# A planner that passes backward and forward over its plan, paced warm-up products, and a start cut into finer steps

## The chip, the cores and the metric

The kernel runs on one core of a Trainium2 chip. The metric is the device time of one execution in microseconds (us), the median of several. Names of engines: PE is TensorE (matrix products), DVE is VectorE, ACT is ScalarE, POOL is GpSimd, SP is SyncE, which here issues nearly all DMAs.

## The reference

Three layers follow each other. The first is a linear attention with a decaying state, for each batch and head; then come two expert layers on the same 3072 tokens of width 384.

```python
# r, k, v, w: [4, 8, 768, 48]; state: [4, 8, 48, 48]
for t in range(S):
    cur = einsum('bhd,bhe->bhde', u[None] * kt, vt)
    y[:, :, t] = einsum('bhd,bhde->bhe', rt, state + cur)
    state = wt[:, :, :, None] * state + einsum('bhd,bhe->bhde', kt, vt)
# x: the y of all heads side by side, [3072, 384]
x = (silu(x @ w_gate) * (x @ w_val)) @ w_out            # 384 -> 1536 -> 384
h = x @ w_in                                            # 384 -> 1024
solu = h * softmax(h)
x = (solu - mean) / sqrt(var + 1e-6) * g_ln @ w_out2    # 1024 -> 384
```

The expert weights arrive as 64-bit floats. The kernel turns them into 32-bit values on DVE and ACT, and splits weights and activations into a high and a low part (names with h and l: hg and lg, xh and xl, mh and ml), so that each product of matrices is three products on PE: high by high, high by low, low by high.

## The kernel before

**Attention.** The tokens are cut into 24 pieces, n = 0 to 23, of 128 tokens: piece n is token block q = n // 4 of batch b = n % 4, two chunks of 64 tokens each, all 8 heads. `att_prep(n)` (from line 455) records its steps.

- On DVE: a forward scan of w (L484), a reciprocal (L487), a backward scan (L489), then two multiplies of r and k with the results (L337, written to the tile `feat`). For pieces under NDG = 4 one more product r*k goes to the tile `PR` (L337), from r and k as they were before those multiplies. `PR` has one buffer, which all pieces share.
- On PE: `s_kt` transposes k (kT, L574) and, for pieces under 4, multiplies r*k with u in products of two columns (L576, the diagonal step) in the same step and the same PSUM bank; `s_qk` does k by r (QK, L527); `s_up` k by v (UP, L633); `s_av` the masked QK by v and r by the state (AV, L676 and L679). Pieces under NFLAT = 4 are *flat*: QK and UP are steps of their own, with one bank each, one mask product and one add to the state on DVE. From piece 4 on, QK and UP are one step over two banks, with three mask products and two adds.
- On ACT: the transposed k goes to `kt` (L340), the diagonal from PSUM to `dg` and, for pieces under NOWN = 4, eight products with it (L590, called own here), with pieces from NOWN to NDG on DVE.
- At the end PE transposes the result (yT, L726), and ACT and DVE split it into `xh` and `xl`.

**First expert layer.** `weights` loads and decodes two 128-column weight tiles at a time (steps L340, L376, L379, L382, L384); for the first two loads (NLO = 1) PE forms the low halves with the identity matrix (the corrections, L449 and L450). `moe1_unit` does a unit m of 128 of the 1536 columns for one token block: 9 products for gate, 9 for value, silu on ACT, the product on DVE, the split into `mh` and `ml`, and 9 products with w_out (L748 to L750). Units m < HM0 = 3 of block 0 and m < HM1 = 6 of block 1 run in two halves of 256 tokens, so that they can start when two pieces of four are ready; the others in one of 512.

**Second expert layer.** Products L1028 to L1030, then a softmax and a normalization on DVE and ACT, a transpose by DMA for most pieces, and products L1197 to L1199. `finish` copies each result from PSUM on ACT and stores it with a DMA from SP.

**What sets the order.** Nothing is issued as it is written. Every step goes into a `Graph` with an engine, an estimated duration, a priority (a due time) and its data; `emit` then plays the plan through once: each engine takes, of its steps that are ready by the estimates, the one with the smallest priority, and the instruction is issued at that moment. So the estimates and the due times fix each engine's order; on the chip an engine goes through its own order and waits where its data are not there. The due times come from the tables of numbers in line 63. While PE has nothing to do at the start, `fill` puts in products of the identity matrix with itself (L1234, the warm-ups); before, these are 13 products at the start.

Of the kernel before, what the change touches and what calls it, by code (L numbers as in the profile page):

```python
# [26 lines left out]
C = 64  # L27
# [14 lines left out]
NFLAT = 4  # L42
# [5 lines left out]
NOWN = 4  # L48
# [12 lines left out]
T0, ADV, ADV2, MARG = 15.0, 2.0, 12.0, 16.0  # L61
HM0, HM1 = 3, 6
ATS, PPS, OWS, DUS, DUD, UNS, SIS, FWS, FRS = {2: -2.0, 3: -1.0, 5: -8.0, 7: -3.0, 8: 4.0, 10: 5.0, 11: 1.0}, {0: 2.0, 1: 5.0, 2: -1.0, 4: 2.0, 5: -5.0, 6: 1.0, 7: 3.0, 9: 5.0, 10: -4.0, 11: 13.0}, {1: -29.0, 2: 2.0, 3: 5.0}, {1: -1.0, 2: 2.0, 6: -2.0, 7: -9.0, 8: -22.0, 9: -8.0, 10: -4.0, 11: 2.0, 12: 1.0, 14: 8.0, 16: -12.0, 17: -9.0}, {0: -12.0, 3: 10.0, 4: -3.0, 5: 14.0, 6: -5.0, 7: -7.0, 8: -22.0, 10: 12.0, 11: 6.0, 12: 7.0, 13: -2.0, 14: -14.0, 15: 3.0, 16: 41.0, 17: 1.0}, {0: 14.0, 1: 6.0, 2: -8.0, 3: -4.0, 4: 1.0, 6: 9.0, 7: 6.0, 9: -3.0}, {0: -9.0, 1: -5.0, 2: 10.0, 3: 9.0, 5: -16.0, 7: -27.0, 8: -4.0, 9: 16.0}, {3: 16.0, 4: 1.0, 5: -8.0, 7: 18.0, 8: -12.0, 9: -19.0}, {1: -31.0, 2: 2.0, 4: -2.0, 6: -1.0, 7: -1.0, 8: -8.0, 9: -1.0}
# [9 lines left out]
class Graph:  # L73
# [5 lines left out]
    FILL, FROM, UNTIL, WARM, IDLE = 0.235, 4.0, 8.4, 7.0, 2.2  # L79
    LAT = {"PE": 0.2, "ACT": 0.13, "DVE": 0.13, "POOL": 0.13, "DMA": 2.6, "ADMA": 2.6, "CTL": 0.0}  # L80

    def __init__(self):
        self.opts, self.prio, self.fn, self.deps = [], [], [], []
        self.last, self.readers = {}, {}
        self.port = set()
        self.fill = self.tiles = None
        self.takes, self.holds, self.bank_of, self.owner = {}, {}, {}, {}
# [52 lines left out]
    def emit(self):  # L140
        self.order_takes()
        n = len(self.opts)
        users = [[] for _ in range(n)]
# [11 lines left out]
        self.at, self.fills = [None] * n, []  # L155
        free = sorted(self.tiles)
        idle = [0.0]

        def fill(m, t):
            if not free or t < self.FROM or t > self.UNTIL and t < idle[0] + self.IDLE:  # L160
                return 0.0
            for _ in range(m):
# [29 lines left out]
        while events:  # L192
            t = events[0][0]
            while events and events[0][0] <= t:
                _, kind, i = heapq.heappop(events)
                if kind == 0:
                    for e in self.opts[i]:
                        heapq.heappush(ready.setdefault(e, []), (self.prio[i], i))
# [11 lines left out]
                else:  # L210
                    for j in users[i]:
                        same = taken[i] == "PE" and "PE" in self.opts[j]
                        ready_at[j] = max(ready_at[j], t + (0.0 if same else self.LAT[taken[i]]))
# [1104 lines left out]
```

## Time and profile before

| | us |
|---|---|
| timed runs | 742.65, 743.68, 746.32 |
| median | 743.68 |
| the profiled execution | 744.02 |
| its span | 741.9 |
| busy in the span: PE / DVE / ACT / POOL | 730.9 / 546.0 / 356.5 / 72.6 |

The profile is of one execution. The span goes from the first to the last instruction; the time of the execution has what lies around it. The busy time of an engine is a sum over stages with different limits, so it is read stretch by stretch. The granted clock of PE is given as a share of 2.4 GHz; the two levels seen are 1.00 and 0.50. A start in the order of time is in us from the span's start, the figure behind it is how long the instruction (or the merged group) took, and a bracket tells how long the engine was idle before it and what ended that.

### The profile page before, as it was taken

Reading aid. Unit: us, or ns where it says so; the run is one execution under the profiler, and the core shown is the slowest. Engines: PE = TensorE matmul, PEld = TensorE weight load, DVE = VectorE, ACT = ScalarE, POOL = GpSimd, SP = SyncE. Lnnn points to the kernel's source line nnn. Section 1 sums busy time; section 2 is a strip of 40 time slices with the busy share of each in tenths; the row PEclk is TensorE's granted clock in tenths of the full one; section 3 lists DMA queues with packets and bytes.
Section 4 is the critical chain, followed back from the end, with each engine's and each line's share of the span. In section 5 each row is a group of like instructions: output and inputs, shape, how many; then the busy total and the mean of one; then the engine's idle time right before and its main releaser. Section 6 shows DMA issues by size and latency. Waiting matters only on the chain.

```text
span 741.9 us, 15891 instructions
## 1 busy us (share of the span) xinstructions
PE 730.9 (99%) x6287; PEld 632.1 (85%) x6287; DVE 546.0 (74%) x1099; ACT 356.5 (48%) x698; POOL 72.6 (10%) x64
## 2 busy tenths in 40 slices
PE   6999999999999999999999999999999999999998
PEld 6798888999888888888888888888888889999998
DVE  7699999988877687766867537976344988778830
ACT  4797673634344333323434323564554465555551
POOL 0000000000000000000000000000024242543240
PEclk9699999999999999999999999999999999999999
DMA  9887642414333233333333125610324244343331
GB/s 266 255 250 222 222 142 82 137 47 130 106 116 106 60 85 103 115 91 89 96 88 123 47 57 143 198 43 12 89 58 149 64 122 116 88 114 96 86 106 43
DMA packets 62617, 84.63 MB, mean 114 GB/s; under 512 B 18896, under 2 KB 46288, under 8 KB 62544
## 3 DMA queue, kind: packets, MB, share of 16 engines
q1 hardware_dynamic: 62128, 83.52, 39.3%
q8 instruction: 49, 0.80, 0.5%
q14 instruction: 24, 0.20, 0.1%
q10 hardware_dynamic: 416, 0.10, 0.1%
HBM read 59.47 MB, written 9.44 MB: 93 GB/s over the span
## 4 chain that ended last, share of the span: by engine, by line
PE 99%; DMA 0%; issue 0%; DVE 0%; ACT 0%
PE ps L748 17%; PE ps L749 16%; PE ps L750 16%; PE hp L1028 4%; PE hp L1029 4%; PE hp L1030 4%; PE psa L748 4%; PE psa L750 4%; PE psa L749 4%; PE pc L1199 2%; PE pb L1199 2%; PE pb L1197 2%; PE pc L1197 2%; PE pb L1198 2%; PE pc L1198 2%; PE ps L676 2%
## 5 line engine op out<-in xcount | busy, mean ns | idle before, releaser
L748 PE MATMUL ps<-xh,hg 128*128 128x512 f32 (+1 forms) x348 | 130.5, 375 | 0.0
L750 PE MATMUL ps<-xh,lg 128*128 128x512 f32 (+1 forms) x348 | 128.9, 370 | 0.0
L749 PE MATMUL ps<-xl,hg 128*128 128x512 f32 (+1 forms) x348 | 128.8, 370 | 0.0
L337 POOL TENSOR_TENSOR tl<-xt,th 128x512 fp32r<-128x512 f32 x44 | 55.7, 1296 | 636.0 <-DVE ml L337 543.9
L340 ACT ACTIVATE mh<-sg 128x512 fp32r<-128x512 f32 (+1 forms) x81 | 47.1, 583 | 92.9 <-DVE sg L337 88.1
L748 PE MATMUL ps<-mh,ho 128*128 128x512 f32 (+1 forms) x243 | 90.0, 370 | 0.0
L749 PE MATMUL ps<-ml,ho 128*128 128x512 f32 (+1 forms) x243 | 88.9, 366 | 0.0
L750 PE MATMUL ps<-mh,lo 128*128 128x512 f32 (+1 forms) x243 | 88.9, 366 | 0.0
L748 PEld LDWEIGHTS ps<-xh,hg 128*128 128x128 f32 x348 | 65.6, 188 | 11.5
L750 PEld LDWEIGHTS ps<-xh,lg 128*128 128x128 f32 x348 | 65.6, 188 | 11.3
L749 PEld LDWEIGHTS ps<-xl,hg 128*128 128x128 f32 x348 | 65.6, 188 | 10.8
L785 ACT ACTIVATE sg<-ps 128x512 f32<-128x512 f32 (+1 forms) x57 | 32.1, 563 | 84.9 <-PE ps L750 82.8
L337 DVE TENSOR_TENSOR sg<-sg,ps 128x512 f32<-128x512 f32 (+1 forms) x59 | 37.2, 630 | 47.4 <-PE ps L750 46.4
L337 DVE TENSOR_TENSOR ml<-sg,mh 128x512 fp32r<-128x512 f32 (+1 forms) x81 | 50.4, 623 | 16.5 <-ACT mh L340 16.3
L1029 PE MATMUL hp<-i2l,xh 128*128 128x512 f32 x144 | 56.6, 393 | 0.0
L1028 PE MATMUL hp<-i2h,xh 128*128 128x512 f32 x144 | 56.5, 393 | 0.0
L1030 PE MATMUL hp<-i2h,xl 128*128 128x512 f32 x144 | 56.0, 389 | 0.0
L340 ACT ACTIVATE kt<-PR 32x256 f32<-32x256 f32 (+1 forms) x128 | 46.3, 361 | 17.3 <-DVE PR L600 15.8
L748 PEld LDWEIGHTS ps<-mh,ho 128*128 128x128 f32 x243 | 45.8, 188 | 7.5
L750 PEld LDWEIGHTS ps<-mh,lo 128*128 128x128 f32 x243 | 45.8, 188 | 7.4
L749 PEld LDWEIGHTS ps<-ml,ho 128*128 128x128 f32 x243 | 45.8, 189 | 7.2
L1040 DVE TENSOR_REDUCE sm<-hp 128x1 f32<-128x1024 f32 x24 | 29.3, 1221 | 29.8 <-PE hp L1030 29.8
(184 smaller groups left out, 1683.9 us busy)
## 6 DMA issues: line engine op xcount, KB each, us to landing
tok<-tok SPq DMA_DIRECT2D x20, 576.0 KB, 4.2
xt<-tb SPq DMA_DIRECT2D x176, 64.0 KB, 2.0
feat<-feat SPq DMA_DIRECT2D x24, 448.0 KB, 4.4
feat<-feat SPq DMA_DIRECT2D x24, 231.4 KB, 3.0
vv<-vv SPq DMA_DIRECT2D x24, 192.0 KB, 4.7
st<-w_gate SPq DMA_DIRECT2D x12, 384.0 KB, 5.2
st<-w_val SPq DMA_DIRECT2D x12, 384.0 KB, 5.9
st<-w_out SPq DMA_DIRECT2D x12, 384.0 KB, 4.1
```

Source lines behind the costliest of these rows:

```text
L337: return lambda: eng.tensor_tensor(out=out, in0=in0, in1=in1, op=op)
L340: return lambda: ACT.activation(out=out, in_=in_, func=AF.Copy)
L748: PE.matmul(out=o, lhsT=wh, rhs=xhi, start=first, stop=False, **kw)
L749: PE.matmul(out=o, lhsT=wh, rhs=xlo, start=False, stop=False, **kw)
L750: PE.matmul(out=o, lhsT=wl, rhs=xhi, start=False, stop=last, **kw)
L785: lambda: ACT.activation(out=sg, in_=pg.t[:, 0:n], func=AF.Silu), [pg.key], [sk]))
L1028: PE.matmul(out=hp()[:, f], lhsT=xh_[:, k, s], rhs=R["i2h"][:, k, f], start=(k == 0), stop=False)
L1029: PE.matmul(out=hp()[:, f], lhsT=xh_[:, k, s], rhs=R["i2l"][:, k, f], start=False, stop=False)
L1030: PE.matmul(out=hp()[:, f], lhsT=xl_[:, k, s], rhs=R["i2h"][:, k, f], start=False, stop=(k == KD - 1))
L1197: PE.matmul(out=po(), lhsT=th[:, m], rhs=R["o2h"][:, m], start=(m == 0), stop=False)
L1198: PE.matmul(out=po(), lhsT=th[:, m], rhs=R["o2l"][:, m], start=False, stop=False)
L1199: PE.matmul(out=po(), lhsT=tl[:, m], rhs=R["o2h"][:, m], start=False, stop=(m == M2 - 1))
```

## The change

- The planner. `emit` now makes a plan with the given due times (`run`), goes backward over it from its end (`late`: when must each step begin at the latest, with each engine doing one thing at a time), takes these times as new due times, and does so three times; the plan with the earliest planned end is issued. A DMA is planned as a time to be issued, then a place on a shared wire, then a landing.
- The warm-ups. The planner keeps an account of how much PE has done in the last stretch of the plan, with a weight for each kind of step (`cool`: 0.05 for the diagonal step, 0.35 to 0.55 for small products, 0.9 otherwise). Up to 60 us of the plan it puts a warm-up product in when the account is low and PE has nothing ready, and below a second bound it holds back a step that is ready and puts a warm-up first. There are now 18 warm-ups: 8 at the start, then 4, 1, 1, 2 and 2.
- The start. w of pieces 0 and 1 comes in two halves, each with a scan of its own. `PR` has two buffers, one for each parity of n. The diagonal step is a step of its own, with a bank of its own and a due time of its own.
- Numbers: NFLAT 4 to 5, NOWN 4 to 3, HM1 6 to 4, T0 15 to 17, and new tables of due times. PEV, ARO and NSH are 0, so what hangs on them emits nothing.
- The end. The result of the last piece is copied in two halves, on ACT and on DVE, and stored by two DMAs, from SP and from ACT.

```diff
-NFLAT = 4
+NFLAT = 5
-NOWN = 4
+NOWN = 3
-T0, ADV, ADV2, MARG = 15.0, 2.0, 12.0, 16.0
-HM0, HM1 = 3, 6
+T0, ADV, ADV2, MARG = 17.0, 2.0, 12.0, 16.0
+HM0, HM1 = 3, 4
+NSPL = 2
+PEV, ARO = 0, 0
+ROUNDS = 3
+NSH = 0
...
-    FILL, FROM, UNTIL, WARM, IDLE = 0.235, 4.0, 8.4, 7.0, 2.2
-    LAT = {"PE": 0.2, "ACT": 0.13, "DVE": 0.13, "POOL": 0.13, "DMA": 2.6, "ADMA": 2.6, "CTL": 0.0}
+    FILL, FROM, UNTIL, WARM, SPAN, HEAT, COLD = 0.235, 4.0, 8.4, 7.0, 3.4, 1.3, 1.1
+    LAT = {"PE": 0.2, "ACT": 0.13, "DVE": 0.13, "POOL": 0.13, "DMA": 1.3, "ADMA": 1.3, "CTL": 0.0}
+    ISSUE, GEN = 0.45, 0.95
...
     def emit(self):
         self.order_takes()
+        self.uses = [b.users for b in self.bank_of.values()]
+        prio = list(self.prio)
+        best = self.run(prio, False), prio
+        for _ in range(ROUNDS):
+            prio = self.late()
+            end = self.run(prio, False)
+            if end < best[0]:
+                best = end, prio
+        self.run(best[1], True)
...
+    def late(self):
...
+            for e, heap in ready.items():
+                if heap and not busy.get(e):
+                    i = heapq.heappop(heap)[1]
+                    busy[e] = True
+                    end = t + self.took[i]
+                    begin[i] = last - end - (self.GEN if e == "DMA" else 0.0)
+                    heapq.heappush(events, (end, 1, i))
+        return [self.prio[i] if self.at[i][0] == "CTL" else begin[i] for i in range(n)]
...
+        def heat(t):
+            while recent and recent[0][1] < t - self.SPAN:
+                recent.pop(0)
+            return sum((b - max(a, t - self.SPAN)) * c for a, b, c in recent)
 
         def fill(m, t):
-            if not free or t < self.FROM or t > self.UNTIL and t < idle[0] + self.IDLE:
+            if not free or not self.FROM < t < 60.0 or t > self.UNTIL and heat(t) > self.HEAT:
                 return 0.0
...
-                i = None if busy.get(e) else first(heap)
+                i = None if busy.get(e) or e == "PE" and self.UNTIL < t < 60 and free and heat(t) < self.COLD else first(heap)
...
-    PR = slots(atp, "PR", [128, H, C], 1)
+    PR = slots(atp, "PR", [128, H, C], 2)
...
-        g.add("DVE", 1.17, pp, lambda: DVE.tensor_tensor_scan(
-            out=e, data0=w[:, 0:WC], data1=pat_f, initial=0.0, op0=ALU.mult, op1=ALU.add),
-            [("fw", i), "pat_f"], ["e"], port=True)
+        for z, (c0, c1) in enumerate(zip(cut, cut[1:])):
+            g.add("DVE", 0.62 if two else 1.17, pp, lambda c0=c0, c1=c1: DVE.tensor_tensor_scan(
+                out=e[:, c0:c1], data0=w[:, c0:c1], data1=pat_f[:, c0:c1], initial=0.0, op0=ALU.mult, op1=ALU.add),
+                ([fw[z]] if two else fw) + ["pat_f"], [ek[z]] if two else ek, port=True)
...
-                for j in range(HP if n < NDG else 0):
+
+            g.add("PE", 0.43, pr, fn, fk + ["ident"], take=[ps])
+            psd = g.bank(ALL) if n < NDG else ps
...
+            def diag():
+                for j in range(HP):
                     PE.matmul(out=dg()[:, j::HP], lhsT=pair(pr_, j), rhs=u_sb[:, 2 * j:2 * j + 2], start=True, stop=True,
                               skip_group_check=True)
 
-            g.add("PE", 1.3 if n < NDG else 0.38, pr, fn, fk + ["ident"] + (["pr", "u"] if n < NDG else []), take=[ps])
+            if n < NDG:
+                g.cool[g.add("PE", 0.9, pr + DGS.get(n, 0.0), diag, [("pr", i), "u"], take=[psd])] = 0.05
...
+        h, free = DM // 2, g.readers.get(("ob", jb), ())
+        g.add("ACT", t_act(h), p0 + 20, lambda: copy(R["ob"][jb][:, 0:h], po()[:, 0:h])(), [pk, ("p2", 5)], [("ob", jb)])
+        g.add("DVE", t_dve(h), p0 + 20, lambda: DVE.tensor_copy(out=R["ob"][jb][:, h:], in_=po()[:, h:]), [pk, ("p2", 5)],
+              [("ob", "tail")], after=free)
...
```

Three places show what moves. The first is DVE's start, piece 0 and the beginning of piece 1, before. `e` is the forward scan's result; feat_189 is w, r and k of piece 0 and feat_190 those of piece 1 (after: feat_190 and feat_191); AM is the masked QK, zt a small product for the state.

```order
L484 SCALAR_TENSOR_TENSOR e_195<-feat_189,pat_f 112x528
L487 RECIPROCAL pat_r<-e_195 112x16
L337 TENSOR_TENSOR PR_176<-feat_189 112x512
L489 SCALAR_TENSOR_TENSOR feat_189<-feat_189,pat_r 112x528
L337 TENSOR_TENSOR zt_198<-e_195 112x4
L337 TENSOR_TENSOR PR_176<-feat_190 112x512
L337 TENSOR_TENSOR feat_189<-feat_189,e_195 112x16x32
L337 TENSOR_TENSOR feat_189<-feat_189 112x16x32
```

The same place after the change:

```order
L559 SCALAR_TENSOR_TENSOR e_196<-feat_190,pat_f 112x264 x2
L562 RECIPROCAL pat_r<-e_196 112x16
L405 TENSOR_TENSOR zt_199<-e_196 112x4
L564 SCALAR_TENSOR_TENSOR feat_190<-feat_190,pat_r 112x528
L405 TENSOR_TENSOR PR_176<-feat_190 112x512
L405 TENSOR_TENSOR feat_190<-feat_190,e_196 112x16x32
L405 TENSOR_TENSOR feat_190<-feat_190 112x16x32
L559 SCALAR_TENSOR_TENSOR e_196<-feat_191,pat_f 112x264 x2
L405 TENSOR_TENSOR PR_177<-feat_191 112x512
```

The r*k product of piece 1 no longer stands ahead of the two multiplies of piece 0, and that of piece 0 stands behind its back scan.

The second place is PE's start, before: warm-ups, then transpose, diagonal step, QK and UP of piece 0.

```order
L1234 MATMUL ps_99<-ident 128x128 x13
L574 MATMUL ps_99<-ident,feat_189 128x112 x4
L576 MATMUL ps_99<-u_sb,PR_176 128x2 x4
L527 MATMUL ps_100<-feat_189 64x64 x16
L633 MATMUL ps_101<-vv_191,kt_196 64x48
```

After, down to the first product of UP 0:

```order
L1342 MATMUL ps_99<-ident 128x128 x8
L646 MATMUL ps_99<-ident,feat_190 128x112 x4
L602 MATMUL ps_100<-feat_190 64x64 x16
L656 MATMUL ps_101<-u_sb,PR_176 128x2 x4
L656 MATMUL psa_105<-u_sb,PR_177 128x2 x4
L1342 MATMUL psa_106<-ident 128x128 x4
L714 MATMUL psa_106<-vv_192,kt_197 64x48
```

Five warm-ups fewer at the start, the diagonal steps of pieces 0 and 1 behind QK 0, and four warm-ups ahead of UP 0.

The third place is on PE too, where the first gate products of the first expert layer begin, before. xh_116, hg_126 and lg_127 are x and the first gate weights; st are the decoded weights.

```order
L726 MATMUL psa_105<-ident,tok_194 128x128 x3
L449 MATMUL psa_106<-st_162,ident 128x384
L450 MATMUL psa_106<-hg_126,nident 128x384
L449 MATMUL ps_101<-st_162,ident 128x384
L450 MATMUL ps_101<-hg_126,nident 128x384
L737 MATMUL psa_105<-xh_116,nident 128x128 x3
L449 MATMUL ps_100<-st_163,ident 128x384
L450 MATMUL ps_100<-ho_128,nident 128x384
L449 MATMUL ps_99<-st_163,ident 128x384
L450 MATMUL ps_99<-ho_128,nident 128x384
L527 MATMUL psa_106<-feat_189 64x64 x16
L574 MATMUL psa_105<-ident,feat_189 128x112 x4
```

Behind these rows come the diagonal step of piece 2 and the first gate product. After:

```order
L1342 MATMUL ps_99<-ident 128x128 x2
L824 MATMUL ps_99<-ident,tok_195 128x128 x3
L835 MATMUL ps_100<-xh_116,nident 128x128 x3
L1342 MATMUL psa_105<-ident 128x128 x2
L835 MATMUL ps_99<-xh_116,nident 128x128 x3
L517 MATMUL psa_105<-st_162,ident 128x384
L518 MATMUL psa_105<-hg_126,nident 128x384
L517 MATMUL ps_101<-st_162,ident 128x384
L518 MATMUL ps_101<-hg_126,nident 128x384
L846 MATMUL psa_106<-xh_116,hg_126 128x256
```

The gate products stand ahead of the second pair of corrections (st_163) and of the QK, transpose and diagonal step of piece 2; four warm-ups stand between the steps for x.

## Rows read from the trace of the kernel before

**Rows 1.** By stretches: busy us of PE, PEld, DVE, ACT, POOL; clock; DMA share; GB/s.

```profile
core 0 of [0], span 741.9 us
0.00:7.12 7.12, 3.02 (x14) 3.02 (x15) 4.09 (x7) 1.80 (x3) 1.59 (x8) 1.00 0.77 209
7.12:17.36 10.24, 7.50 (x136) 7.04 (x138) 9.12 (x19) 5.18 (x19) 0.00 (x0) 1.00 1.02 301
17.36:31.01 13.65, 12.87 (x157) 10.29 (x153) 10.07 (x22) 10.07 (x23) 0.00 (x0) 0.50 0.92 256
38.00:160.00 122.00, 122.00 (x1518) 108.73 (x1515) 119.16 (x254) 77.65 (x157) 0.00 (x0) 1.00 0.54 166
160.00:200.00 40.00, 40.00 (x525) 35.43 (x524) 33.43 (x74) 17.67 (x45) 0.00 (x0) 1.00 0.34 91
```

**Rows 2.** PE in order of time: start, us, operation, idle before.

```profile
10.59 0.57 PE L574 MATMUL ps<-ident,feat 112*128 112x112 f32 x4 [1.90 <-issue]
...
15.12 0.57 PE L574 MATMUL psa<-ident,feat 112*128 112x112 f32 x4 [0.81 <-issue]
...
20.57 1.94 PE L633 MATMUL psa<-vv,kt 64*64 64x48 f32 x32
...
31.48 0.83 PE L449 MATMUL ps<-st,ident 128*128 128x384 f32 x2
...
32.42 1.15 PE L527 MATMUL psa<-feat 48*64 48x64 f32 x32
33.50 0.60 PE L574 MATMUL psa<-ident,feat 112*128 112x112 f32 x4
33.94 0.96 PE L576 MATMUL psa<-u_sb,PR 112*128 112x2 f32 x8
34.76 0.36 PE L748 MATMUL ps<-xh,hg 128*128 128x256 f32 x1
...
35.08 0.28 PE L750 MATMUL ps<-xh,lg 128*128 128x256 f32 x1
...
36.88 0.28 PE L750 MATMUL ps<-xh,lg 128*128 128x256 f32 x1
37.09 1.07 PE L633 MATMUL ps<-vv,kt 64*64 64x48 f32 x31
```

**Rows 3.** DVE in order of time, first piece.

```profile
3.95 1.26 DVE L484 TENSOR_TENSOR_SCAN e<-feat,pat_f 112x528 f32<-112x528 f32 x1 [1.83 <-DMA feat<-feat]
...
6.22 1.25 DVE L489 TENSOR_TENSOR_SCAN feat<-feat,pat_r 112x528 f32<-112x528 f32 x1
...
8.59 0.69 DVE L337 TENSOR_TENSOR PR<-feat 112x512 f32<-112x512 f32 x1 [1.06 <-DMA feat<-feat]
...
9.80 0.69 DVE L337 TENSOR_TENSOR feat<-feat 112x512 f32<-112x512 f32 x1
```

**Rows 4.** DMA issues on the page: count, KB each, us to landing.

```profile
tok<-tok SPq DMA_DIRECT2D x256, 12.0 KB, 1.8
```

**Rows 5.** ACT in order of time, first pieces.

```profile
12.00 1.36 ACT L340 ACTIVATE kt<-ps 64x192 f32<-64x192 f32 x4
...
13.59 1.91 ACT L590 ACTIVATE tok<-tok,dg 128x48 f32<-128x48 f32 x8
...
23.76 0.92 ACT L382 ACTIVATE st<-tb 128x768 int32<-128x768 int8 x1
```

**Rows 6.** PE in order of time, fused QK and UP.

```profile
60.61 0.69 PE L527 MATMUL ps<-feat 48*64 48x64 f32 x32
...
61.69 0.39 PE L748 MATMUL ps<-mh,ho 128*128 128x256 f32 x1
```

**Rows 7.** PE in order of time, products of 512 columns.

```profile
88.65 0.40 PE L748 MATMUL ps<-mh,ho 128*128 128x512 f32 x1
...
100.92 0.39 PE L748 MATMUL psa<-xh,hg 128*128 128x512 f32 x1
```

**Rows 8.** ACT in order of time, the last copy.

```profile
738.56 0.49 ACT L340 ACTIVATE ob<-pc 128x384 f32<-128x384 f32 x1 [3.62 <-PE pc L1199]
```

More of the change, by code (lines that the diff above doesn't have):

```diff
@@ L211, in emit @@
                     for j in users[i]:
-                        same = taken[i] == "PE" and "PE" in self.opts[j]
-                        ready_at[j] = max(ready_at[j], t + (0.0 if same else self.LAT[taken[i]]))
+                        ready_at[j] = max(ready_at[j], t + self.lag(taken[i], next(iter(self.opts[j]))))
                         left[j] -= 1
@@ L231, in emit @@
                     if e == "PE":
-                        idle[0] = end
+                        recent.append((t, end, self.cool.get(i, 0.9)))
                     heapq.heappush(events, (end, 1, i))
@@ L609, in s_kt_dve @@
                 for a in range(2):
-                    g.add("ACT", 0.72, pr, lambda p=p, a=a: [move(p, a, z) for z in range(2)], ["pr"], [("kt", i, p, a)])
+                    g.add("ACT", 0.72, pr, lambda p=p, a=a: [move(p, a, z) for z in range(2)], [("pr", i)], [("kt", i, p, a)])
         rk = tk[:, 0].rearrange("p h d -> p (h d)")
@@ L651, in s_up @@
                 g.add("DVE", 0.34, pr, tt(DVE, ro, ro, bc(0), ALU.mult), [("zt", i, 0)], [("ro", i)], port=True)
+            elif n < ARO:
+                g.add("ACT", 0.72, pr, lambda: [ACT.activation(
+                    out=ro[:, j], in_=u(0)[0:112, j], func=AF.Copy, scale=zt[:, 0, j:j + 1]) for j in range(HP)],
+                      [keys[0], ("zt", i, 0)], [("ro", i)])
             else:
@@ L670, in y, with own @@
                 return ps[p].t[:, 0:HP * D].rearrange("p (j d) -> p j d", j=HP)
+            def own(p):
+                x = tk[:, 1, HP * p:HP * p + HP].rearrange("p h d -> p (h d)")
+                PE.matmul(out=ps[p].t[:, 0:HP * D], lhsT=ident, rhs=x, start=True, stop=False, skip_group_check=True)
             def fn():
                 cp = [(c, p) for c in range(2) for p in range(2)]
+                for p in range(2 if n < PEV else 0):
+                    own(p)
                 for j in range(HP):
                     for c, p in cp:
-                        PE.matmul(out=y(p)[rows[c], j], lhsT=am[rows[p], c, j], rhs=v[rows[p], c, j], start=True,
+                        PE.matmul(out=y(p)[rows[c], j], lhsT=am[rows[p], c, j], rhs=v[rows[p], c, j], start=n >= PEV,
                                   stop=c == 0 and q == 0, skip_group_check=True)
```

132 lines of the change are left out of this document (94 added, 38 removed).

## The prediction

> **What bounds the kernel now.** I read the granted clock and the engines' busy time by stretches first, then the order of time of VectorE (DVE), TensorE (PE) and ScalarE (ACT) in the first 40 us, and last one stretch of the middle. The profiled execution took 744.02 us, its span 741.9 [rows 1], so 2.1 us lie around the span; the median of the three timed runs, 743.68, is 0.3 lower.
>
> The stretches fall into three parts [rows 1]. From 38 us to 160 PE is busy 122.00 of 122.00 us at full clock, and DVE 119.16: two engines are full at once. From 160 on PE stays full and DVE has room (33.43 of 40). No order can make PE's work there shorter, only the work itself can. What is not full is the start. PE's first useful product, the transpose of piece 0's keys, starts at 10.59; and from 17.36 to 31.01 the granted clock is 0.50, that is 1.2 GHz, after a stretch of 10.24 us in which PE was busy 7.50. A state update (UP) of 32 products takes 1.94 us in the slow stretch (from 20.57) and 1.07 at full clock (from 37.09) [rows 2]. The first gate product of the first expert layer starts at 34.76 [rows 2]; from there PE never waits. So the change pays only by what it does before that product, by the PE work that it adds or saves, and by the last store.
>
> **The change, part by part.** All times are worked out with the durations of before.
>
> *First piece.* Before, the forward scan of w starts when its data are in, at 3.95, and the second multiply by the scan, which frees PE, ends at 10.49 (9.80 + 0.69). Between them DVE waits 1.06 us and spends 0.6 on the r*k product of piece 1, because PR has one buffer and that product stands ahead of the multiplies [rows 3]. After, w comes in two halves and the order is half scan, half scan, reciprocal, back scan, r*k, two multiplies. The second half cannot land sooner than the whole did, so 3.95 stays; half a scan of 1.25 is 0.65, to 4.6; reciprocal and the small product 0.35, to 4.95; back scan 1.17 (6.22 to the next start; an end overlaps a start by 0.08), to 6.1; r*k 0.6; two multiplies 1.2, to 8.0. PE starts at 8.1 in place of 10.59. Bounds: 7.6 if the first half lands 0.4 sooner and all hand-overs are tight, 9.0 if the extra DMA issue and its landing cost 0.9.
>
> *Second piece.* DVE goes on with two half scans (1.2), r*k of piece 1 and its reciprocal (0.8), the mask product of piece 0 (0.6), back scan and two multiplies (2.4): 13.2, so PE's transpose of piece 1 starts at 13.3 and not at 15.12 [rows 2]. Its r and k make 1.49 MB with all that is issued before them; 209 GB/s have moved that by 7.12 [rows 1], and with the 1.8 us that even 12 KB take to land [rows 4] they are in at about 9.0, in time. PE meanwhile does QK 0 (1.08, 32.42 to 33.50), the two diagonal steps (0.82 each, 33.94 to 34.76), which no longer hold up the keys' evacuation, four warm-up products and UP 0. A warm-up is two of the 14 products in the 3.02 us before the clock rises [rows 1], 0.43; at full clock I take half of that, 0.22. UP 0 ends at 13.1, QK 1 at 14.8, AV 0 (taken as long as UP, 1.1) at 15.9.
>
> *UP 1 to the first gate product.* UP 1 needs v of piece 1, which SP now issues behind two pairs of weights and issued ahead of them before: 3.66 MB in all; at 301 GB/s after 7.12 [rows 1] it has moved at 14.3 and lands at about 16.3. Behind the waiting UP 1 stand on PE the transpose of x of piece 0 and AV 1, and for these ACT and DVE wait. UP 1 runs to 17.4, AV 1 to 19.2. ACT has kt 0 (1.36), own 0 (1.91), a weight step, kt 1, two weight steps, and own 1 from 17.4 to 19.3 [rows 5]. Behind it stand eight instructions before the low half of the first weight: four weight steps of 0.9 and four copies of x of 0.45 (0.49 for 384 columns [rows 8], less the overlap), 5.4 us; with the low half 25.2, and with a step and the other half 26.6. The transpose of piece 1 on PE (20.1 to 20.6) feeds this row in time. So the first gate product starts at 25.2 and the value product ends at 27.7.
>
> *Equal work.* Before, PE had by 37.09 done the same two products, and also the second pair of weight corrections and QK, transpose and diagonal step of piece 2. After, these follow: 0.94 each for the corrections (31.48 to 32.42), 0.82, 0.45 and 1.08: 4.2 us, PE at 31.9. The gain at equal work is 5.2 us.
>
> *PE's own work.* Piece 4 becomes flat: its QK and UP run apart, 1.08 + 0.95 (1.07 less the overlap), where the fused form takes 1.08 from 60.61 to 61.69 [rows 6]: 0.95 lost. HM1 falls from 6 to 4, so two units run in whole width: 15 products of 256 columns take 1.80 (35.08 to 36.88) [rows 2], 0.120 each, and 54 of 512 take 12.27 (88.65 to 100.92, no other work between) [rows 7], 0.227 each. A unit of 27 products in two halves is 6.48, whole 6.13: 0.35 saved, 0.7 for two. Net 0.25 lost: 4.95.
>
> *DVE's side.* DVE has no room from 38 to 160, so PE can keep a gain only if DVE's queue moves too. DVE is idle 7.7 us up to 31.01 (3.03, 1.12 and 3.58 [rows 1]). In the chain above I count about 4 left, most of it before the first half of w: 3.7 gained. Its work shrinks: three mask products become one, two state adds one, four instructions in the two whole units fall away, one (own of piece 3, moved from ACT) is added. Instructions of 512 columns take 0.6 to 0.7 [rows 3], smaller ones most of that, so about 1 us, an estimate. DVE moves by 4.7, a little less than PE would, so 4.7 counts; its bounds are nothing (the waits stay) and 8.7 (all of them go).
>
> *Tail.* The last copy of 384 columns takes 0.49 on ACT [rows 8]; halved over ACT and DVE it saves at most 0.25, and the two stores run beside each other. I take 0.1, bounds -0.3 (the store on ACT's queue issues late) to 0.25.
>
> *The rest of the order.* Backward and forward passes move instructions everywhere, but from 160 on PE does its products in nearly the same sequence, and its waits are zero before; it can lose here, not gain. I take nothing. PEV, ARO and NSH are 0 and emit nothing. The two more DMAs for w cost SP one issue each before 3.9, when its queue has issued all that the DMA engines can move; without that cover, 0.4 each.
>
> Sum: 4.7 + 0.1 = 4.8; 744.02 - 4.8 = 739.2 for the profiled execution, 738.9 against the median. I say 739.1.
>
> **The clock.** All this takes the clock at full level from about 7 us on. Before, it rose at 7.12 during the first warm-ups and fell at 17.36, after UP 0, a wait of 0.81, a diagonal step of two-column products and a QK [rows 1, 2]. After, the eight first warm-ups end at about 7.4, a wait of 0.7 follows, and ten more stand between the small products until the weights come. That more wide products stand where it fell speaks for a clock that holds; that the stretch from 8 to 25 is still small products with waits speaks against. The Trainium skill (TensorE: Matmul & The Clock Gate, Part 1) says that the observation is free-running and does not start anew with the kernel, so the moment of a change varies from run to run. By that, warm-ups at fixed places would catch it in some executions and not in others; the three runs, 742.65 to 746.32, leave room for this but do not show it. That is the first rival.
>
> **Rivals.**
> 1. *The clock falls all the same* at about 10 to 17 us and rises only with the weight products. For: the start stays sparse. Against: the ten products. Price: UP 0 and UP 1 each +0.9 [rows 2]; AV and QK by the same doubling about +0.9 each, three of them on the chain; warm-ups +0.9; the corrections before the first product +0.9 each; of these 7 us some 3 run in waits that are there anyway. Gain 0.8: 742.9.
> 2. *DVE becomes the bound* between 38 and 160: its waits for DMA and PE at the start remain, only half of the 3.7 and some 0.6 of the saved work count, 2.5 in all; PE then shows waits there that it does not have now. 741.2.
> 3. *Slower.* The pause between the last first warm-up (7.4) and the transpose (8.1) comes before the clock has risen, and it stays at 1.2 GHz until the gate products. QK 0 is then 2.1, both diagonal steps 1.6, four warm-ups 1.7, UP 0 1.9, kT 1 and QK 1 3, AV 0 1.8, UP 1 1.9, AV 1 1.8, two transposes of x 1.9 and six single warm-ups 2.6, two corrections 3.8; with 0.9 for the first transpose, 8.1 becomes 33.1 for the first gate product. If the clock then rises, the two products end at 35.3 and the equal work at 39.5, against 37.09: 2.4 lost, 0.25 in work: 746.3. The place is the granted clock at 8 us; above 32 us for the first gate product this case is decided.
>
> **How the numbers follow.** Forecast 0.60 (own range 737.0 to 741.2), rival 1 0.23, rival 2 0.10, rival 3 0.07. A difference under 0.5% (3.7 us: under 740.0 or over 747.4) is about what a measurement of this kernel cannot tell from none. The forecast lies at 739.1, 0.9 from that bound, so three quarters of it count as faster: 0.45, and 0.05 for rival 2 and starts better than worked out; slower by so much needs rival 3 with another mishap, and gets 0.06; the same 0.44. The range runs from 735.8 (the first piece at 7.6, DVE's larger bound) to 743.4, which takes in rivals 1 and 2 and leaves out rival 3.
>
> **What would show it.** Granted clock 1.00 from 7 to 38; first transpose at 8.1, transpose of piece 1 at 13.3, UP 1 at 16.4 waiting for v, first gate product at 25.2 behind ACT; PE without waits from 32 on; DVE full until about 155. Wrong if the clock reads 0.50 in that stretch, if PE waits for DVE between 38 and 160, or if the first gate product comes after 29.

## The result, and the profile after

The changed kernel takes 751.75 us in the median of 12 runs (748.39 to 754.65), the kernel before 743.29 beside it (741.81 to 748.2): ratio 1.0108, interval 1.0085 to 1.0131. It is slower, by 8.5 us; the forecast was 739.1. The profiled execution took 751.5 us, span 749.7. Here and below the ratios leave out six executions that lie far above the others of their kernel (e6: 754.7 and 756.55; e9: 756.16 and 759.27; e13: 1626.02; e11: 1874.88, its profiled one, whose profile is not read), and the medians keep them.

By stretches (busy us of PE, PEld, DVE, ACT, POOL; clock; DMA share; GB/s), against [rows 1]:

```profile
0.00:7.16 7.16, 3.78 (x16) 3.48 (x16) 4.30 (x9) 1.69 (x3) 1.59 (x8) 1.00 0.73 189
7.16:10.57 3.41, 1.69 (x37) 1.51 (x37) 3.38 (x7) 1.01 (x4) 0.00 (x0) 1.00 1.01 292
10.57:17.40 6.83, 6.83 (x55) 6.61 (x56) 3.14 (x7) 3.36 (x12) 0.00 (x0) 0.50 1.07 370
17.40:38.00 20.60, 20.10 (x313) 17.05 (x310) 18.40 (x36) 19.39 (x50) 0.00 (x0) 1.00 0.80 220
38.00:160.00 122.00, 121.78 (x1503) 107.71 (x1500) 118.28 (x251) 73.23 (x140) 0.00 (x0) 1.00 0.55 170
160.00:200.00 40.00, 39.13 (x472) 32.09 (x470) 32.24 (x68) 16.46 (x39) 0.00 (x0) 1.00 0.32 87
200.00:260.00 60.00, 56.49 (x534) 45.11 (x531) 38.96 (x80) 19.38 (x43) 0.00 (x0) 0.97 0.31 86
```

The clock fell here too, but earlier and for less: 0.50 from 10.57 to 17.40, against 17.36 to 31.01. What is new is below: PE, which had no gap from 160 on, lacks 0.87 us up to 200 and 3.51 up to 260, and the clock falls once more (0.97 in the mean).

PE in order of time, the rows that answer to [rows 2]:

```profile
8.88 0.58 PE L646 MATMUL ps<-ident,feat 112*128 112x112 f32 x4 [1.77 <-DVE feat L405]
...
10.47 1.80 PE L656 MATMUL ps<-u_sb,PR 112*128 112x2 f32 x8
12.13 1.85 PE L656 MATMUL psa<-u_sb,PR 112*128 112x2 f32 x8
...
15.82 1.83 PE L714 MATMUL psa<-vv,kt 64*64 64x48 f32 x32
17.58 0.60 PE L646 MATMUL ps<-ident,feat 112*128 112x112 f32 x4
...
20.53 1.13 PE L714 MATMUL ps<-vv,kt 64*64 64x48 f32 x32
...
27.95 0.28 PE L846 MATMUL psa<-xh,hg 128*128 128x256 f32 x1
```

The first gate product starts at 27.95, 6.8 us sooner than before. The waits of PE (us in total, times, longest), those of 0.5 us or more:

```profile
PE ps L1342 <- DMA ident<-eye: 3.3, 1, 3.3
PE ps L846 <- DVE TS L405: 2.4, 1, 2.4
PE ps L646 <- DVE feat L405: 1.8, 1, 1.8
PE ps L847 <- DVE ml L405: 0.9, 2, 0.6
PE ps L846 <- ACT mh L408: 0.6, 1, 0.6
```

To see where the lead went I give every product of PE its duration at full clock, add these up, and compare the times at which a kernel and the profiled kernel before reach the same sum. Worked out from the PE rows of each trace, minus is ahead:

```
at (before, us)                     35      84     182     251
changed kernel                    -2.8    -0.7    +0.1    +8.3
e1  no passes                     +1.3    +5.6    +6.7    +7.9
e2  loads early                   +3.0    +4.8    +5.6   +11.7
e3  loads on GpSimd               +2.9    +5.1    +6.0    +7.3
e4  no passes, no paced           -3.1    +4.1    +4.8    +6.4
e5  13 first warm-ups             -5.8    -3.7    -3.0    +3.0
e6  e3 with 13                    -0.7    +1.5    +2.7    +3.4
e9  e3 with 18                    -4.5    -2.3    -1.5    +4.6
e13 half transposes, 13           -4.1    -1.9    -1.2    -1.0
e14 no passes, 13                 -5.5    -1.1    +0.4    +0.9
e15 half transposes, 18           -0.5    +1.6    +2.2    +2.4
e16 e15, dense                    -4.1    -2.0    -1.4    -1.2
e7  before with 8                 +4.8    +4.8    +5.6    +5.6
e8  before with 18                -1.1    -1.1    -1.1    -1.1
```

(At 35 the kernels have done different shares of the small work. From 84 on one thing is to be kept in mind: by this measure the changed kernel has 0.7 us less to do, the two units of block 1 in whole width, which the kernel before does in halves between 125 and 180 us. At 182 and 251 it is therefore 0.7 further than its row says.) Two columns matter. From 182 to 251 the changed kernel loses 8.2 us. And the column at 84, the start, goes from -3.7 to +5.1 among kernels whose PE has the same order (e5 and e3).

**Where the 8.2 us go.** SP's queue in order of time (start, us, what it issued, how often):

```profile
184.41 0.35 SPq L411 DMA_DIRECT2D tok<-tok  x1
191.86 0.33 SPq L411 DMA_DIRECT2D feat<-feat  x1
196.86 6.71 SPq L411 DMA_DIRECT2D tok<-tok  x9
203.67 0.52 SPq L411 DMA_DIRECT2D feat<-feat  x1
204.24 0.43 SPq L411 DMA_DIRECT2D vv<-vv  x1
204.71 14.97 SPq L411 DMA_DIRECT2D tok<-tok  x23
219.78 0.52 SPq L411 DMA_DIRECT2D feat<-feat  x1
220.40 0.37 SPq L411 DMA_DIRECT2D tok<-tok  x1
```

A piece's y is transposed by 16 transfers of 12 KB (tok<-tok in rows of many); a single tok<-tok is a load of 576 KB. The queue stands from 184.8 to 191.9 and to 196.9 behind issues whose buffers are not free, and then issues two pieces' 32 transposing transfers with one pair of loads between them: 21.7 us, about 0.63 each where nothing holds them. Only behind them, at 220.40, comes the load of tok. Before, each 16 had the next loads behind them:

```profile
185.81 11.66 SPq L343 DMA_DIRECT2D tok<-tok  x17
197.56 1.51 SPq L343 DMA_DIRECT2D feat<-feat  x1
199.12 0.42 SPq L343 DMA_DIRECT2D vv<-vv  x1
199.66 11.71 SPq L343 DMA_DIRECT2D tok<-tok  x17
211.41 5.06 SPq L343 DMA_DIRECT2D feat<-feat  x3
```

The chain of waits of the changed kernel goes on from there:

```profile
220.40 6.61 DMA tok<-tok
227.03 0.57 DVE tok L405
227.62 0.36 DVE TS L405
227.98 0.47 DVE tok L405
228.48 0.36 DVE TS L405
228.88 0.69 PE ps L846
```

The load lands at 227.03; DVE, in order, does its two products of tok around the state adds, and PE waits 2.4 us for the second TS. Behind that wait the granted clock is 0.50 for 3.41 us. The wait and the half clock are about 4.5 of the 8.2, by the starts of PE's products; about 3.2 more are shorter pauses between 191 and 223, where PE waits for mh, ml and x. That these hang on the row too isn't seen in this trace; e13 below shows it.

### The profile page after: what moved, and what is told of

It is laid out like the page before. It is cut to its first block, busy times and chain, and to the rows that moved or that the text cites. A ratio compares the mean times of both kernels' runs of the same rounds, so it can differ in the third digit from the quotient of the medians.

```text
span 749.7 us, 15778 instructions
## 1 busy us (share of the span) xinstructions
PE 736.1 (98%) x6243; PEld 631.7 (84%) x6243; DVE 548.0 (73%) x1096; ACT 353.7 (47%) x685; POOL 72.5 (10%) x64
## 4 chain that ended last, share of the span: by engine, by line
PE 89%; DMA 4%; SPq 2%; DVE 2%; ACT 2%; issue 1%; POOL 0%; ACTq 0%; DVEq 0%; POOLq 0%
PE ps L846 15%; PE ps L847 15%; PE ps L848 14%; PE hp L1127 4%; PE hp L1126 4%; PE hp L1128 4%; PE psa L846 4%; PE psa L848 3%; PE psa L847 3%; PE pb L1297 2%; PE pc L1297 2%; PE pb L1295 2%; DMA feat<-feat 2%; PE pc L1295 2%; PE pb L1296 2%; PE pc L1296 2%
## 5 line engine op out<-in xcount | busy, mean ns | idle before, releaser
L846 PE MATMUL ps<-xh,hg 128*128 128x512 f32 (+1 forms) x327 | 125.5, 384 | 2.7 <-DVE TS L405 2.4
L847 PE MATMUL ps<-xl,hg 128*128 128x512 f32 (+1 forms) x327 | 123.9, 379 | 0.1
L848 PE MATMUL ps<-xh,lg 128*128 128x512 f32 (+1 forms) x327 | 123.7, 378 | 0.0
L846 PEld LDWEIGHTS ps<-xh,hg 128*128 128x128 f32 x327 | 61.9, 189 | 15.1 <-DVE TS L405 2.9
L848 PEld LDWEIGHTS ps<-xh,lg 128*128 128x128 f32 x327 | 62.0, 189 | 11.4
L847 PEld LDWEIGHTS ps<-xl,hg 128*128 128x128 f32 x327 | 62.0, 190 | 11.2 <-DVE xl L405 0.4
L405 DVE TENSOR_TENSOR sg<-sg,ps 128x512 f32<-128x512 f32 (+1 forms) x56 | 35.5, 635 | 40.5 <-PE ps L848 39.0
L846 PE MATMUL psa<-xh,hg 128*128 128x512 f32 (+1 forms) x147 | 53.9, 367 | 0.1
L847 PE MATMUL psa<-xl,hg 128*128 128x512 f32 (+1 forms) x147 | 53.0, 360 | 0.2 <-DVE xl L405 0.2
L848 PE MATMUL psa<-xh,lg 128*128 128x512 f32 (+1 forms) x147 | 53.0, 360 | 0.1
```

The lines of the kernel that those rows point to most:

```text
L405: return lambda: eng.tensor_tensor(out=out, in0=in0, in1=in1, op=op)
L846: PE.matmul(out=o, lhsT=wh, rhs=xhi, start=first, stop=False, **kw)
L847: PE.matmul(out=o, lhsT=wh, rhs=xlo, start=False, stop=False, **kw)
L848: PE.matmul(out=o, lhsT=wl, rhs=xhi, start=False, stop=last, **kw)
```

## The experiments

All are timed beside the kernel before; the times are medians in us, then the ratios with their intervals in brackets. Edits are shown in short.

### e1 to e4: the passes, the loads, the paced warm-ups

e1: `ROUNDS = 0`.

> The changed kernel with ROUNDS = 0: the plan is the first forward run, by the due times written in the tables; all other edits stay. Theory A (the backward passes give the loads of the later pieces due times just in time, and on SP's queue they come to stand behind up to 32 transposing transfers of 0.6 us each; PE loses 8.5 us between 182 and 260): 740 to 743, no wait of PE and no fall of the clock between 180 and 260. Theory B (what is lost is lost at the start: half clock from 10.57 to 17.40, transpose of piece 1 late): about 751, as the start stays. Theory C (the passes cost time by the order of PE, DVE and ACT, not by SP's queue): 740 to 743 as well.

e2, in `late`, `soon` being the four loads of each piece:

```
-begin[i]
+begin[i] - 12.0 * (i in self.soon and begin[i] > 100)
```

> The changed kernel, passes and all, but the due times that the backward pass gives to the four loads of a piece (w, r and k, v, tok) are taken 12 us earlier from 100 us of the plan on; the start is the same instruction for instruction. Theory A (loads late behind transposes on SP): 743 to 745, the 2.44 us wait of PE at 228.88 and the half clock behind it gone. Theory B (start): 751. Theory C (order of the engines' own work): 749 to 751, since that order moves little.

e3, for the same four loads:

```
-nc.sync.dma_start(out=out, in_=in_)
+(nc.gpsimd if n >= 6 else nc.sync).dma_start(out=out, in_=in_)
```

> The changed kernel with its order on every engine, but the loads of pieces 6 to 23 are issued by GpSimd's queue instead of SP's, so that no transposing transfer stands ahead of them. Theory A (SP's queue): 741 to 745, tok of the piece in question lands before 215 instead of 227.01, no PE wait at 228.88. Theory C (order of PE, DVE, ACT): 749 to 751 with the same waits. Theory B (start): 751.

e4: e1 with `HEAT, COLD = -1.0, 0.0`.

> As the run without passes, and without paced warm-ups after 8.4 us (neither filler products nor small products held back for the count); the eight first ones stay. If the paced warm-ups hold the clock up or bring it back early (it rose at 17.40 in the changed kernel and at 31.01 before): the clock falls near 10 us and rises only with the gate products, first gate product 1 to 3 us later than with them, 1 to 3 us slower than the run without passes. Rival (they only stand in the way of the transpose of piece 1 on PE's queue): the transpose of piece 1 moves from about 17.6 to 14 to 15, and the time falls by 1 to 2 us.

Measured: e1 749.91, 1.0092 [1.0061, 1.0124]; e2 754.46, 1.0153 [1.0125, 1.0181]; e3 750.27, 1.0083 [1.0051, 1.0116]; e4 751.42, 1.0126 [1.0091, 1.0161]. By the times alone theory A had fallen: none came near 743. The table says otherwise, for e3 at least. From 182 to 251 e1 and e3 lose 1.2 and 1.3 us where the changed kernel lost 8.2; but their starts were 5.6 and 5.1 behind at 84, where its profile was 0.7 ahead, and a PE that comes later also finds more of its data ready. e3's PE is busy 99.40 of the 100 us from 160 to 260. Its start, with the same instructions on PE in the same order as the changed kernel's:

```profile
9.78 0.98 PE L649 MATMUL ps<-ident,feat 112*128 112x112 f32 x4 [2.55 <-DVE feat L405]
10.69 1.97 PE L605 MATMUL ps<-feat 48*64 48x64 f32 x32
...
18.01 1.94 PE L717 MATMUL psa<-vv,kt 64*64 64x48 f32 x32
19.88 1.01 PE L649 MATMUL ps<-ident,feat 112*128 112x112 f32 x4
...
33.63 0.28 PE L849 MATMUL psa<-xh,hg 128*128 128x256 f32 x1
```

Every step takes the time of 1.2 GHz (QK 1.97 against 1.15 at full clock), and the first change of the granted clock in this trace, and in e2's, is its rise at 28.93 (28.68). Three executions of one start: a rise at 7.16, 28.68 and 28.93. The Trainium skill (TensorE: Matmul & The Clock Gate, Part 1) says that the observation is free-running and does not start anew with a kernel. These three agree with it in that the moment varies, by over 21 us; that this is the reason no run here shows. So there were two causes, and a second theory, D: with eight first warm-ups the clock often doesn't rise at the start. e3's own times fit it: two executions at 745.70 and 746.07, four at 749.62 to 751.55.

e2 is no cure: it lost 6.1 us in the same stretch. On SP its early loads wait for buffers still in use, and the transposing transfers wait behind them. e4 started like the changed kernel (-3.1), then PE ran out of weights (it waits 1.1 us for hg and 0.8 for lg between 44 and 48, and the clock is half from 47.60 to 51.01). What the paced products are worth this doesn't show: between 35 and 84 it loses 7.2 us where e1, and e14 below, lose 4.3 and 4.4 with them, but its first half clock (10.05 to 20.29) was shorter than e1's (9.74 to 23.39) and its interval overlaps e1's.

### e5 to e8: the number of first warm-ups

One line, emitting some of the first products twice (in e7, leaving five out); e5 is the changed kernel with 13, e6 the same on top of e3, e7 and e8 are the kernel before with 8 and 18:

```
-for _ in range(m if real else 0):
+for _ in range((1 + (len(self.fills) < 5)) * m if real else 0):
```

> The changed kernel with 13 first warm-up products (26 rows of PE) ahead of the first transpose, as the kernel before has, instead of 8 (16 rows); everything else in the same order. Theory D (eight are too few: in many executions the clock has not risen when they end, stays at 1.2 GHz until about 29 us, and PE is some 5 us behind by 50 us, as in the profiles of the two runs with other loads; the profiled execution of the changed kernel was a lucky one): the clock reads 1.00 from 7 to 10 us, the spread of the times narrows and the median falls by 1 to 3 us, to 749 to 751; not further, since the loads on SP's queue (theory A) still cost 6 to 8 us between 182 and 260. Rival (the number of first warm-ups does not matter; the start loses by its small products at the low level): 751 to 753.

> Loads of pieces 6 to 23 on GpSimd's queue and 13 first warm-ups, both. Theories A and D together: the loss after 160 us is 1 to 2 us and the start comes out as in the profile of the changed kernel: 744 to 746, against 750.27 with the loads alone. Rival to D: 749 to 751.

> The kernel before with 8 first warm-up products instead of 13, nothing else. Theory D: in part of the executions the clock does not rise before the first transposes; 2 to 4 us slower, 745 to 747, more spread. Rival: within 1 us of before.

> The kernel before with 18 first warm-up products instead of 13; PE waits 2.17 us ahead of its first transpose there, and five at the half clock take 2.2. Theory D: 13 are nearly enough, so within 1 us of before, or up to 2 us faster if the fall at 17.36 comes later. Rival: within 0.5 us.

Measured: e5 751.04, 1.0097 [1.0065, 1.0128]; e6 745.11, 1.0021 [0.9995, 1.0048]; e7 746.51, 1.0031 [1.0011, 1.0051]; e8 742.34, 0.9994 [0.9976, 1.0012]. D holds where the late loss doesn't hide it: five warm-ups fewer cost the kernel before 3.1 us of median (746.51 beside 743.39), five more change nothing that can be told, and with the loads off SP's queue five more take 5.2 us off the changed kernel (750.27 to 745.11). With the loads on SP they take 0.7, inside the noise (e5 just missed its 749 to 751): what PE gains at the start it waits for at 188 to 230. e5's profile shows this best, since its clock rose at 8.10 and held to the end. PE in order of time:

```profile
9.05 0.57 PE L646 MATMUL ps<-ident,feat 112*128 112x112 f32 x4 [0.23 <-issue]
...
14.57 0.60 PE L646 MATMUL ps<-ident,feat 112*128 112x112 f32 x4
...
17.52 1.13 PE L714 MATMUL ps<-vv,kt 64*64 64x48 f32 x32
...
25.00 0.28 PE L846 MATMUL psa<-xh,hg 128*128 128x256 f32 x1
```

It was 3.0 us ahead at 182 and 3.0 behind at 251; this execution took 746.51, the other five 750.48 to 752.47.

### e9 to e12: more of the start, and a control

e9 is e6 with 18 first warm-ups; e10 is e9 with `NFLAT = 4`; e11 is e9 with each paced warm-up doubled; e12 is e8 with its loads of pieces 6 to 23 on GpSimd as in e3.

> Loads of pieces 6 to 23 on GpSimd's queue and 18 first warm-ups (13 before this). PE waits 1.0 to 1.3 us ahead of its first transpose with 13, five more at the full clock take 1.1. If the clock falls at about 13 us because that gap and the two diagonal steps follow the warm-ups: it falls later or not at all, as in the profile of the changed kernel with 13, where it held, and the median goes from 745.1 to 741 to 743. Rival (only the phase decides, and PE's own start is 1 us later when the clock rises late): 744.5 to 746.

> As the run with 18 and the loads on GpSimd, with NFLAT = 4 as before (piece 4 is fused again). The forecast put the flat piece 4 at 0.95 us lost, and every profile since shows PE lose about 0.95 at the same work, near 50 to 56 us. If that is a loss of PE's own work: 0.9 us faster than with NFLAT = 5. Rival (flat pieces spare DVE, which is full there, and the planner's new order costs as much): the same or slower.

> As the run with 18 and the loads on GpSimd, and each paced warm-up after them doubled (8 instead of 4 between the diagonal steps and the first state update, 22 instead of 11 in all). If denser warm-ups hold the clock: no fall before the gate products, 740 to 742. Rival (they only delay PE's queue: some 11 products more, 0.22 us each at full clock, 2.4 us): the run with 18 plus 1 to 2.5 us.

> A control: the kernel before with 18 first warm-ups and its loads of pieces 6 to 23 on GpSimd's queue. Theory A (what this queue gave the changed kernel is the wait behind the transposing transfers, which the order before does not have): within 1 us of the run of before with 18, 741.5 to 743.5. Rival (loads on GpSimd are better whatever the order, by their own queue's share of the DMA engines): 2 us or more faster.

Measured: e9 747.7, 1.007 [1.0041, 1.0099]; e10 756.39, 1.0164 [1.0125, 1.0203]; e11 747.19, 1.0065 [1.004, 1.0091]; e12 743.89, 1.0001 [0.9978, 1.0024]. The control, 0.4 us over its range and 1.6 over e8, speaks for theory A against its rival: the other queue gives nothing to the order before, whose loads stand behind 16 transposing transfers and not behind 32. e9, e10 and e11 contradicted me; e11 is level with e9, and by its count it had 20 paced warm-ups (40 rows of PE) in place of 10, not 22 in place of 11 as I had written. e9 was 1.5 us ahead at 182 and 4.6 behind at 251. SP's row there, and the end of the chain of waits:

```profile
193.63 23.52 SPq L411 DMA_DIRECT2D tok<-tok  x32
...
215.61 4.43 DMA tok<-tok
...
220.38 0.53 ACT xh L408
...
220.95 0.67 PE ps L849
```

No load stands on this queue any more; the row of transposing transfers itself is late, and ACT's split of x (xh) waits for the last of them. In e6, whose PE came 4 us later, 0.7 was lost. So the loads were only a part of it: with them gone the row of issues itself is the bound there. How large a part stays open: by the medians moving the loads took 5.9 us off at 13 warm-ups (751.04 to 745.11), by the profiles e9 loses 6.1 where e5, with its loads on SP, lost 6.0. e10's new plan waited 5.1 us at the same place, so its time says nothing on the flat piece.

### e13 to e16: the row of transposing transfers

e13 is e5 with every second of them on GpSimd's queue, the loads on SP; e14 is e1 with 13 first warm-ups; e15 is e13 with 18; e16 is e15 with each paced warm-up doubled.

```
-dma(yx[...], yb[...])
+td(yx[...], yb[...], a)    # (nc.gpsimd if a % 2 else nc.sync).dma_start
```

> The changed kernel with 13 first warm-ups, its loads on SP as they are, but every second of the transposing transfers of 12 KB issued by GpSimd's queue, so that SP's row per piece is 8 issues instead of 16. If the row of 0.63 us issues is what makes tok and x late between 182 and 260: the wait of about 2.4 us for TS near 228 goes and the loss after 160 us falls from 6.7 to 8.5 us to under 3; 744 to 747, against 751.04 with the row whole. Rival (the transfers wait for DVE, and their issue costs nothing by itself): 750 to 752.

> The run without the passes, with 13 first warm-ups instead of 8: its profile had lost 5.7 us by 60 us at the half clock and 2.2 after that. If the start's loss was the clock that rose late and fell: 744 to 747, level with the run with both GpSimd loads and 13 (745.11), and the passes' part of the loss is then the difference to 751.04. Rival (the start's own order, with due times meant for other plans, loses it): 749 to 751.

> As the run with every second transposing transfer on GpSimd, with 18 first warm-ups instead of 13. With the stretch after 160 us mended, the time is the start's: its profile had the clock rise at 9.33 and fall from 12.74 to 16.16, and was 0.95 us ahead of the kernel before at the end. If five more warm-ups make the rise safer: 744 to 745.5, against 745.88, and less spread. Rival (the fall after the diagonal steps decides): 745.5 to 747.

> As the run with 18, and each paced warm-up after them doubled. If the clock holds then (the run with both and the loads on GpSimd showed a mean clock of 0.99 to 1.00 in its timed runs), the start's 5 us against the half clock are there in most executions, less up to 2.4 us for 11 more products: 740 to 743, faster than the kernel before. Rival (the products take what the clock gives): 744 to 747.

Measured: e13 745.88, 1.0036 [1.001, 1.0062]; e14 748.03, 1.0063 [1.0041, 1.0084]; e15 745.0, 1.0007 [0.9985, 1.0029]; e16 742.77, 0.9987 [0.9968, 1.0007]. e13's SP queue where the changed kernel's stood still:

```profile
187.46 0.33 SPq L411 DMA_DIRECT2D feat<-feat  x1
192.45 3.05 SPq L414 DMA_DIRECT2D tok<-tok  x5
197.51 0.33 SPq L411 DMA_DIRECT2D feat<-feat  x1
197.89 1.56 SPq L411 DMA_DIRECT2D vv<-vv  x1
199.49 6.85 SPq L414 DMA_DIRECT2D tok<-tok  x11
206.44 0.53 SPq L411 DMA_DIRECT2D feat<-feat  x1
209.29 0.35 SPq L411 DMA_DIRECT2D tok<-tok  x1
```

The load of tok goes out at 209.29 instead of 220.40, PE shows no wait of 0.2 us or more from 100 to 300, and from 182 to 251 the kernel loses nothing (-1.2 to -1.0), where e9, about as far ahead at 182 (-1.5), lost 6.1. The Trainium skill (DMA: Bandwidth & Descriptors, Issuing engines are not separate DMA queues) says that issuing from several engines saves only the time to initiate a transfer, usually small beside the transfer. Here one issue is indeed smaller, 0.63 us against 1.8 to the landing [rows 4], but 16 issues take 10 us, and what is queued behind them is held as long; that time was worth 5.2 us of median (e5 to e13). The measurement decides.

e14 missed its range of 744 to 747: without the passes, and with the tables left as they are, 3.0 us better than e5, not 6. Its profile is of its fastest execution (743.80; the others 746.60 to 751.75). On its SP the loads stand behind 16 transposing transfers, as before the change:

```profile
188.20 10.01 SPq L411 DMA_DIRECT2D tok<-tok  x16
198.32 1.39 SPq L411 DMA_DIRECT2D feat<-feat  x2
```

e15, 0.9 us below e13, came out in its range, but the intervals overlap. e16 adds the clock: with 18 first and 20 paced warm-ups it rose at 8.11 and stayed, and 12 times lay within 741.77 to 743.53, where e13's (without the 1626.02) went from 741.11 to 748.55. It came out in its range, but not faster than the kernel before: it is the best form of the changed kernel found, level with it.

### e17 and e18: the old start with a held clock

The kernel before with 18 first warm-ups, and one (e17) or two (e18) more behind nearly every PE step up to 30 us:

```
 self.fn[i](e)
+for _ in range(1 if e == "PE" and free and self.UNTIL < t < 30.0 else 0):
+    self.fill(self.tiles[free[0]])
```

> The kernel before with 18 first warm-ups and one more warm-up product behind nearly every step of PE up to about 30 us (18 in all), nothing else. If the start's clock is what separates the executions of the kernel before (738.8 to 748 us at 743.2): the half clock from 17.36 to 31.01 shrinks or goes, the spread narrows and the median falls to 739 to 741. Rival (the products take what the clock gives, 18 at 0.22 us, 4 us where PE has no wait to hide them): 743 to 746.

> As the run before it with two such products behind each step (36 in all). If one is too little to hold the clock and PE's waits hide two: 739 to 741 and the narrower of the two spreads. Rival (two cost more than the clock gives): 1 to 4 us slower than with one.

Measured: e17 743.04, 0.9982 [0.996, 1.0004], from 741.87 to 743.42; e18 746.22, 1.0032 [1.0011, 1.0053]. The clock held in both profiles (rise at 7.61 and 8.15). e17 missed its 739 to 741: the spread narrowed, the median stayed. By the rows of PE it has 19 added products and e18 38: 19 take about what the clock gives, 38 take more (3.2 us over e17). No version beat the kernel before by more than can be told.

## Why the prediction was wrong

**The step that failed** is "The rest of the order": "from 160 on PE does its products in nearly the same sequence, and its waits are zero before; it can lose here, not gain. I take nothing." The sequence of PE's products was indeed nearly the same; SP's was not, and I did not read it there. The term measured 8.2 us lost in the changed kernel's profile (6.0 in e5); of the 12.3 between 739.2 and the profiled 751.5 it is the largest part, and about 3.5 more lie before 84. e13 shows the cause: 6 us come back when SP's row of issues is halved, with no other change. The medians say the same: 751.04 (e5) to 745.88 (e13), 5.2 us. That the passes are what ordered SP so is shown by e14, which starts level with the changed kernel at 182 and loses 0.5 there (e1, with a later PE, 1.2). For v of piece 1 the prediction had counted what SP issues ahead of it; for the loads after 160 it did not.

**The clock.** The forecast took it at full from 7 us on, with 0.23 for a fall and 0.07 for a start without a rise. The fall came in the profiled execution (10.57 to 17.40), and the start without a rise in two of three with the same order (e2, e3); rival 3's place, its half-clock steps and its first gate product (33.1 worked out, 33.63 in e3) were right, its chance far too small. Its price was too small as well: 2.4 worked out at equal work, 3.4 with the flat piece 4, and 5.1 behind at 84 in e3. Rival 1 is near what the profiled execution did up to 84: a fall within its 10 to 17 us, 0.7 ahead for the 0.8 that it gave. I saw that five warm-ups fewer ended earlier and left a gap, and still gave it 0.07.

**The start, where the clock holds.** e5 is this case: first gate product 25.00 for 25.2, transpose of piece 1 at 14.57 for 13.3, UP 1 at 17.52 for 16.4. The first transpose came at 9.05 for 8.1: DVE waited 0.75 us for r and k ahead of its r*k product (in the changed kernel 0.67, with the landing at 6.67 and the transpose at 8.88), a wait that the sum left out. UP 1 did not wait for v, which in the changed kernel landed at 15.31, for a UP 1 at 20.53. The lead was 3.7 at 84, where 4.25 was worked out (5.2 less 0.95 for the flat piece; the 0.7 of the whole units comes later): the mechanism was right, the term 0.5 to 0.6 too large. Six of the ten paced products had no price in it, 0.22 each; that they are the difference isn't shown.

**PE's own work, DVE, tail.** The flat piece 4 costs about what was worked out from [rows 6]: in e6 its QK (from 55.24) takes 1.15 us and its UP (from 62.26) 1.13, each alone, while e10 with NFLAT = 4 does both from 55.77 to 56.85. The 0.7 for the two units in whole width doesn't show: at PE's last product e13 and e16 are 1.8 and 2.0 ahead, as at 84 (1.9 and 2.0), though their list is 0.7 shorter; no wait of PE explains it, and why stays open. Rival 2 did not come: PE is busy 121.78 of 122 us from 38 to 160. From the end of PE to the end of the span are 3.35 us, before 3.39: the 0.1 for the tail can't be told from nothing.

**The base.** I set the gain against one profile of the kernel before that had 13.65 us at the half clock, so part of the gain was only a clock that holds. e17 gives the old order that clock, and it ends level with e16 (743.04 and 742.77). What is left to the changed kernel, mended, is the 0.3 between them, which these runs can't tell from nothing. The times of the kernel before, taken beside e1 to e18, say more: nine of 137 have a granted clock of 1.00, and these took 738.65 to 740.62, median 738.90, with no product added. The best of the mended forms at 1.00 are 741.11 (e13, with 23 warm-ups where the kernel before has 13) and 741.77 (e16, with 38). So where the clock holds by itself, the old order already has the forecast's 739.1, and in these few executions it is some 2 us faster than the new one with its warm-ups.

**The sum.** From 751.75: 0.7 for 13 warm-ups, 5.2 for the halved row, 0.9 for 18, 2.2 for the dense ones: 742.77. These are medians taken beside different executions of the kernel before, and the steps of 0.7 and 0.9 are inside the noise. The 3.7 left to the forecast of 739.1 are mostly in e16's profiled execution (742.35): about 2.2 by 84 (2.0 ahead for 4.25, with the price of the added warm-ups in it), 0.7 for the whole units, and 0.4 at the end, where from PE's last product to the end of the span are 3.74 us instead of 3.39. One bound was wrong from the start: with the first piece at 7.6 PE itself gains 5.7 at most, tail included, so DVE's 8.7 could not give the range's lower end of 735.8.

## What to carry to other kernels

When a planner moves work, compare the order of the queue that issues transfers before that of the engines: count its issues between two loads, times the issue time in the trace, and ask what stands behind them. Here the passes put two pieces' rows of small transfers ahead of one load; taking the loads 12 us earlier did not help (e2), halving the row did (e13). And where the start's clock differs from execution to execution, one profile of a start is one draw: compare spreads and several profiles before a lead at the start is entered in a sum.

## What the runs showed of the hardware

- A transposing transfer of 12 KB costs SP about 0.63 us of issue back to back (16 in 10.01 us in e14), more than the 0.3 to 0.5 of a load of 192 to 576 KB.
- The same instructions ran at 1.2 GHz until 28.7 and 28.9 us in two executions; in a third the clock rose at 7.16. The trace's clock row has no entry before the first change: the stretch reads 1.00, and only the durations (QK 1.97 against 1.15) show the level.
- A wait of 2.4 us on PE was followed by 3.41 us at the half clock. The longest waits of e9 (3.7 us) and e10 (5.1) had this second price too, 3.41 us from 221.12 and 6.83 from 222.34, the latter from within the wait; a wait of 2.1 us near 424 in e9 had not.
